# The first batch's attention written out in another order, with its loads and some copies out of PSUM moved

## The chip, the cores and the metric

The kernel runs on one core of one Trainium2 chip. The metric is device time in microseconds (us) of one execution; smaller is better. The core has five engines that run side by side, each through its own list of instructions in order: TensorE (PE, with its weight loads as PEld), VectorE (DVE), ScalarE (ACT), GpSimd (POOL) and SyncE (SP, which here only issues DMA transfers). An instruction that waits for another engine or for a transfer holds up everything behind it on its own engine.

## What is computed

Three layers in fp32, one after the other: a windowed attention, a gated feed-forward layer (FFN), and a mixture of experts. The reference, cut to what matters:

```python
# attention: q, k, v are (4 batches, 8 heads, 576, 64)
rel = pos[:, None] - pos[None, :]
scores = scale * q @ k.T ; scores = where((rel >= 0) & (rel < 64), scores, -1e9)
x = softmax(scores) @ v                      # per batch: 576 x 512
# FFN: w_in 512x1024, conv_w 3x1024, w_out 1024x512
h = maximum(x @ w_in, 0)
conv_out = sum(conv_w[k] * hp[:, k:k + S] for k in range(3))
x = (h * sigmoid(conv_out)) @ w_out
# experts: each row goes to one of 8 experts, chosen by its logits and a running gate
out[b, s] = p[e] * (maximum(x[b, s] @ w1[e], 0) @ w2[e])
```

The FFN's weights arrive as 64-bit floats; integer operations on VectorE turn them into fp32.

## The kernel before

**The stages.** For each batch b there are an attention over four pairs of heads, an FFN first layer `ffn(b)` of eight column blocks f, and output tiles `ffn_out`. The attention of batch b+1 is mixed into the FFN of batch b. The experts follow at the end. Before all that stands the attention of batch 0, which has no FFN to run beside. This document calls it the opening. The FFN of batch 0 begins with the first matmul of L470.

**The opening** is written out by hand as a string of tokens, `FIRST`, which `attention_first` reads from left to right inside a manual schedule. Each token issues its instructions on its engine, so the string sets the order on all engines at once. The digit after the letter is the pair i (0 to 3 are batch 0; 4 is the first pair of batch 1), or, for c, h and u, the chunk of the weight w_in. The second digit is the part g.

| token | work | engine |
|---|---|---|
| T, S, A, V | transposes of k (part 0), q (1) and their rests (2); scores; transposes of the softmax; products with v | PE |
| k, q, t | copies of these transposes out of PSUM | DVE (k, t) and ACT (q) |
| R | mask and row maximum of the scores, reading PSUM | DVE |
| E | exponentials | ACT |
| N, M | the softmax's division, first a third, then the rest | DVE |
| a, x | copies of A and V out of PSUM | ACT |
| l | rest of V's result after rounding, reading PSUM | DVE |
| c | three integer steps on a chunk of w_in (L597, L599, L601) | DVE |
| h, u | rounded chunk; the rest after rounding (L704) | ACT; POOL |
| v, Z | shifted copy of v; clearing of the q buffer of the next batch, after which `load_pair` issues its loads | POOL |
| D | matmuls on constants, which keep PE active | PE |
| w, W, Y | the convolution's taps | DVE, PE, DVE |

**The loads.** `load_pair(b, hp)` issues nine DMAs for a pair (k, q, their rests, v), nearly all on SP's queue; `stage_chunk(i)` loads chunk i of w_in, 512 KB, into a buffer of its own. Before the string is read, pair 0, pair 1, chunks 0 and 1 (on ACT's queue), pair 2, chunk 2, pair 3 and chunk 3 are issued. Eight transfers are outstanding at a time: a DMA on SP waits until the one that stood eight places ahead has landed.

**What the order outside the opening depends on.** The rest of the program is ordered by a scheduler, which can also put instructions of the FFN between those of the opening on an engine whose list has room.

Of the kernel before, what the change touches and what calls it, by code (L numbers as in the profile page):

```python
# [8 lines left out]
F32 = mybir.dt.float32  # L9
# [4 lines left out]
AF = mybir.ActivationFunctionType  # L14
ALU = mybir.AluOpType
# [6 lines left out]
def kernel(  # L22
# [14 lines left out]
    nc = tc.nc  # L37
# [61 lines left out]
    if True:  # L99
# [85 lines left out]
        def stage_T(b, hp, part):  # L185
            qt, kt, ta, v0, v1 = qkv[b, hp]
            qbd, kT = qbds[hp % 2], kTs[hp % 2]
            qT = hb[hp % 2][:, 1:S + 1]
            if b >= TV:

                def turn():
                    if part == 0:
                        nc.vector.transpose(kT, kt)
                    elif part == 1:
                        for h in (0, 64):
                            nc.vector.transpose(qbd[h:h + 64, :, h:h + 64], qt[h:h + 64].rearrange("p (c w) -> p c w", w=W))

                return turn
            ps = bank(b)
            if part == 2:  # L200
                nc.tensor.transpose(ps[:, 0:P], ta.rearrange("p h d -> p (h d)"), ident)

                def evict():
                    nc.vector.tensor_copy(kT[:, 512:576], ps[:, 64:128])
                    if b == 0:
                        nc.vector.tensor_copy(qT[:, 512:576], ps[:, 0:64])
                    else:
                        nc.vector.tensor_copy(qbd[0:64, 8, 0:64], ps[0:64, 0:64])
                        nc.vector.tensor_copy(qbd[64:128, 8, 64:128], ps[64:128, 0:64])

                return evict
            src = (kt, qt)[part]
            for n in range(4):
                nc.tensor.transpose(ps[:, n * P:(n + 1) * P], src[:, n].rearrange("p h d -> p (h d)"), ident)

            def evict():
                if part == 0:
                    nc.vector.tensor_copy(kT[:, 0:512], ps)
                    return
                if b == 0:  # L220
                    nc.scalar.activation(qT[:, 0:512], ps, AF.Copy)
                    return
                pv = ps.rearrange("p (c w) -> p c w", w=W)
                for h in (0, 64):
                    nc.scalar.activation(qbd[h:h + 64, 0:8, h:h + 64], pv[h:h + 64], AF.Copy)

            return evict
# [177 lines left out]
        def attention_first(ORDER, others):  # L405


            later = {}
            for t in ORDER.split():
                s_, i, g = t[0], int(t[1]) if len(t) > 1 else 0, int(t[2]) if len(t) > 2 else 0  # L410
                b, hp = divmod(i, NP)
                if s_ == "T":
                    later["kqt"[g], i] = stage_T(b, hp, g)
                elif s_ == "S":
                    later["R", i, g] = stage_S(b, hp, g)
                elif s_ == "E":
                    stage_E(b, hp, g)
                elif s_ == "N":
                    stage_N(b, hp, ((1, 3),))
                elif s_ == "M":  # L420
                    stage_N(b, hp, ((3, 9),))
                elif s_ == "A":
                    later["a", i, g] = stage_AT(b, hp, g)
                elif s_ == "V":
                    later["x", i, g], later["l", i, g] = stage_AV(b, hp, g)
                elif s_ == "v":
                    shift_v(hp)
                elif s_ in "kqt":
                    later.pop((s_, i))()
                elif s_ in "Raxl":  # L430
                    later.pop((s_, i, g))()
                else:
                    others(s_, i, g)
            assert not later
# [203 lines left out]
        def conv_out(kk):  # L638
# [18 lines left out]
            return finish  # L657

        FIRST = """
            T00 k0 T01 q0 S00 S01 R00 v0 T02 E00 R01 t0 S02 w E01 T10 R02 W T11 k1 E02 c00 T12 t1 c01 q1 v1 N0 S10 S11  # L660
            c02 M0 A00 h0 T20 a00 u0 c10 A01 c11 a01 c12 R10 h1 v2 k2 E10 R11 u1 Y D9 D6 V00 E11 V01 c20 A02 c21 T21
            x00 x01 T22 l00 S12 a02 l01 q2 t2 V02 R12 S20 x02 c22 E12 Z0 T30 l02 T31 R20 T32 S21 h2 N1 v3 E20 S22 M1
            u2 A10 k3 a10 A11 a11 t3 V10 R21 q3 V11 x10 c30 A12 x11 S30 l10 a12 l11 E21 c31 V12 c32 R22 x12 h3 l12 S31
            E22 R30 u3 S32 R31 E30 T40 N2 T41 T42 M2 A20 a20 R32 E31 V20 k4 A21 A22 t4 c40 x20 a21 l20 a22 c41 V21 E32
            V22 c42 c50 x21 N3 x22 q4 l21 l22 h4 M3 D9 D9 A30 a30 u4 c51 V30 A31 c52 x30 A32 a31 l30 a32 V31 h5 V32
            x31 u5 x32 l31 l32 Z1
        """

        with tc.manual_schedule():
# [11 lines left out]
            def stage_chunk(i, eng=nc.sync):  # L681
                c, kk = divmod(i, KD)
                early[c, kk] = load_chunk(st_p.tile([P, CC, 2], U32, name=f"raw{i}"), chunk_in(c, kk), eng)

            for i in range(2):
                stage_chunk(i, nc.scalar)
            for i in range(2, KD):
                load_pair(0, i)
                stage_chunk(i)
            part = {}  # L690

            def others(s_, i, g):

                c, kk = divmod(i, KD)
                fs = slice(c * CC, (c + 1) * CC)
                if s_ == "c":
                    if g == 0:
                        part[i] = cv.tile([P, CC], F32, name="lf")
                    bits64(early[c, kk], part[i], (g,))
                elif s_ == "h":  # L700
                    cin.pop(0)
                    nc.scalar.activation(winH[:, kk, fs], part[i], AF.Copy)
                elif s_ == "u":
                    nc.gpsimd.tensor_tensor(winL[:, kk, fs], part[i], winH[:, kk, fs].bitcast(F32), op=ALU.subtract)  # L704
                elif s_ == "w":
                    part["f"] = cv.tile([P, CC], F32, tag="lf", name="cf")[0:KC, 0:P]
                    bits64(taps, part["f"])
                elif s_ == "W":
                    part["ps"] = bank(0)
                    nc.tensor.transpose(part["ps"][:, 0:KC], part["f"], ident[0:KC, 0:KC])  # L710
                elif s_ == "Y":
                    nc.vector.tensor_copy(cw.rearrange("p k f -> p (k f)"), part["ps"][:, 0:KC])
                elif s_ == "D":
                    warm(bank(0), i)
                else:
                    nc.gpsimd.memset(qbds[i], 0.0)
                    load_pair(1, i)
                    if i == 0:
                        stage_chunk(4)
                        stage_chunk(5)  # L720

            attention_first(FIRST, others)

# [856 lines left out]
```

## Time and profile before

| | |
|---|---|
| median of 3 runs | 627.13 us (625.53 to 628.46) |
| profiled execution | 626.18 us, of which the span shows 624.5 us |
| PE busy | 593.2 us, 95% of the span |
| DVE busy | 431.0 us, 69% |
| ACT busy | 386.9 us, 62% |
| POOL busy | 221.7 us, 36% |
| first matmul of the FFN | 55.79 us after the span's start |

The span runs from the first instruction to the last in one profiled execution. PE is busy nearly throughout; the first 56 us are where it is not. The shares are averages over stages with different limits, so the opening has to be read by itself.

### The profile page before, as it was taken

Reading aid. Unit: us, or ns where it says so; the run is one execution under the profiler, and the core shown is the slowest. Engines: PE = TensorE matmul, PEld = TensorE weight load, DVE = VectorE, ACT = ScalarE, POOL = GpSimd, SP = SyncE. Lnnn points to the kernel's source line nnn. Section 1 sums busy time; section 2 is a strip of 40 time slices with the busy share of each in tenths; the row PEclk is TensorE's granted clock in tenths of the full one; section 3 lists DMA queues with packets and bytes.
Section 4 is the critical chain, followed back from the end, with each engine's and each line's share of the span. In section 5 each row is a group of like instructions: output and inputs, shape, how many; then the busy total and the mean of one; then the engine's idle time right before and its main releaser. Section 6 shows DMA issues by size and latency. Waiting matters only on the chain.

```text
span 624.5 us, 12744 instructions
## 1 busy us (share of the span) xinstructions
PE 593.2 (95%) x4503; PEld 533.9 (85%) x4503; DVE 431.0 (69%) x986; ACT 386.9 (62%) x910; POOL 221.7 (36%) x251
## 2 busy tenths in 40 slices
PE   6779999999999999999999989999999999999996
PEld 4658998899999999989987879979899799897774
DVE  4888999645786167852786977658766686576863
ACT  3567778535876357853661556566765676667863
POOL 3412000001223012342250257458567385643740
PEclk9789999799999999999999999999999999999999
DMA  8794515653245201129102289768668763524850
GB/s 188 187 233 120 165 59 114 111 130 82 53 83 100 70 35 37 35 64 273 46 2 34 93 242 358 265 223 292 218 219 307 247 222 123 179 69 144 295 174 16
DMA packets 122614, 92.17 MB, mean 148 GB/s; under 512 B 96594, under 2 KB 97170, under 8 KB 122544
## 3 DMA queue, kind: packets, MB, share of 16 engines
q1 hardware_dynamic: 116064, 79.61, 44.4%
q0 software_dynamic: 4992, 10.24, 4.9%
q10 hardware_dynamic: 1488, 1.44, 0.8%
q8 instruction: 37, 0.61, 0.4%
q14 instruction: 33, 0.27, 0.1%
HBM read 89.53 MB, written 10.71 MB: 161 GB/s over the span
## 4 chain that ended last, share of the span: by engine, by line
PE 61%; DVE 13%; ACT 9%; DMA 9%; issue 5%; SPq 2%; POOL 0%; POOLq 0%; DVEq 0%; ACTq 0%
PE psM L470 14%; PE psO L512 13%; PE psH L1327 8%; PE psO L1362 8%; PE psA L247 3%; PE psO L1341 3%; ACT x L1168 3%; DMA raw<-in_moe_w_dram 3%; PE psA L324 2%; DMA pcur<-p_dram,gidx 2%; PE psA L299 2%; DMA qk<-in_q_dram 2%; DMA raw<-in_moe_w_out_dram 1%; ACT woutH L1168 1%; PE psG L582 1%
## 5 line engine op out<-in xcount | busy, mean ns | idle before, releaser
L499 POOL TENSOR_TENSOR gL<-h,gH 128x64 fp32r<-128x64 f32 (+5 forms) x46 | 43.6, 956 | 216.0 <-ACT gH L498 209.2
L470 PE MATMUL psM<-x,winH 128*128 128x288 f32 x512 | 108.4, 303 | 0.1
L470 PEld LDWEIGHTS psM<-x,winH 128*128 128x128 f32 x512 | 82.0, 189 | 2.4 <-ACT x L334 0.4
L470 PE MATMUL psM<-x,winL 128*128 128x288 f32 x256 | 76.0, 297 | 0.0
L512 PE MATMUL psO<-woutH,gH 128*128 128x262 f32 (+2 forms) x240 | 64.4, 314 | 1.2 <-ACT gH L498 1.0
L512 PE MATMUL psO<-woutL,gH 128*128 128x262 f32 (+2 forms) x240 | 62.2, 305 | 0.0
L512 PE MATMUL psO<-woutH,gL 128*128 128x262 f32 (+2 forms) x240 | 61.2, 304 | 0.0
L1253 POOL DMA_INDIRECT out_dram<-o,sidx x24 | 31.6, 1319 | 79.6 <-ACT o L1295 41.6
L271 ACT ACTIVATE sS<-sS,mx 128x128 f32<-128x128 f32 (+1 forms) x144 | 55.1, 386 | 6.9 <-DVE mx L259 6.8
L1172 DVE TENSOR_TENSOR woutL<-raw,woutH 128x1024 fp32r<-128x1024 f32 x28 | 33.8, 1224 | 29.1 <-ACT woutH L1168 29.1
L1172 DVE TENSOR_TENSOR x<-raw,x 128x1024 fp32r<-128x1024 f32 x42 | 49.9, 1222 | 4.0 <-ACT x L1168 3.8
L1362 PE MATMUL psO<-gH,x 128*128 128x288 f32 x240 | 51.3, 296 | 0.0
L1327 PE MATMUL psH<-gH,woutH 128*128 128x288 f32 x160 | 48.3, 302 | 0.4 <-DVE gL L1330 0.4
L470 PEld LDWEIGHTS psM<-x,winL 128*128 128x128 f32 x256 | 48.4, 189 | 0.1
L1327 PE MATMUL psH<-gL,woutH 128*128 128x288 f32 x160 | 47.4, 296 | 0.0
L1327 PE MATMUL psH<-gH,woutL 128*128 128x288 f32 x160 | 47.3, 295 | 0.0
L512 PEld LDWEIGHTS psO<-woutH,gH 128*128 128x128 f32 x240 | 41.0, 190 | 4.1 <-ACT gH L498 1.6
L1168 ACT ACTIVATE x<-raw 128x1024 fp32r<-128x1024 f32 x42 | 43.0, 1056 | 0.0
L512 PEld LDWEIGHTS psO<-woutL,gH 128*128 128x128 f32 x240 | 41.4, 191 | 1.4
L512 PEld LDWEIGHTS psO<-woutH,gL 128*128 128x128 f32 x240 | 40.9, 191 | 1.2
L259 DVE CUSTOM_DVE_ANT_0 sS<-psA,mask 128x128 f32<-128x128 f32 (+1 forms) x126 | 28.8, 277 | 17.9 <-PE psA L247 15.1
L1362 PEld LDWEIGHTS psO<-gH,x 128*128 128x128 f32 x240 | 39.8, 189 | 0.0
(395 smaller groups left out, 1645.5 us busy)
## 6 DMA issues: line engine op xcount, KB each, us to landing
raw<-in_moe_w_dram SPq DMA_DIRECT2D x104, 512.0 KB
v<-in_v_dram SPq DMA_DIRECT2D x56, 128.0 KB
y_dram<-ysb SPq DMA_DIRECT2D x17, 256.0 KB
raw<-in_moe_w_out_dram SPq DMA_DIRECT2D x8, 512.0 KB
raw<-in_moe_w_dram SPq DMA_DIRECT2D x32, 128.0 KB
raw<-in_moe_w_in_dram SPq DMA_DIRECT2D x6, 512.0 KB
qk<-in_k_dram SPq DMA_DIRECT2D x32, 72.0 KB
qk<-in_q_dram SPq DMA_DIRECT2D x32, 72.0 KB
```

The source lines that it names most:

```text
L247: nc.tensor.matmul(ps[:, j * P + lo:(j + 1) * P], qbd[:, c, :], kT[:, k0:W * (c + 1)], start=True, stop=True)
L259: nc.vector.tensor_tensor_reduce(sS[:, c, lo:P], ps[:, j * P + lo:(j + 1) * P], mask[:, lo:P], -scale, -NEG, op0=ALU.add, op1=ALU.min, acc ...
L271: nc.scalar.activation(sS[:, c, lo:P], sS[:, c, lo:P], AF.Exp, scale=-1.0, bias=mx[:, c:c + 1], accum_out=sume[:, c:c + 1],)
L470: nc.tensor.matmul(ps[:, 0:HS], wt[:, kk, f * P:(f + 1) * P], xt[:, c0:c0 + HS], start=n == 0, stop=n == 3 * KD - 1,)
L499: e1.tensor_tensor(gL[:, f, r:r + m], t[:, done:done + m], gH[:, f, r:r + m].bitcast(F32), op=ALU.subtract)
L512: nc.tensor.matmul(p_[:, 0:cs.stop - cs.start], gt[:, kk, r:r + P], wt[:, kk, cs], start=n == 0, stop=n == 3 * KF - 1,)
L1168: nc.scalar.activation(dst[kk][0], raws[kk], AF.Copy)
L1172: nc.vector.tensor_tensor(L_, raws[kk], H_.bitcast(F32), op=ALU.subtract)
L1253: nc.gpsimd.indirect_dma_start(out=out[:, :], out_offset=bass.IndirectOffsetOnAxis(ap=sidx[0:n, c:c + 1].bitcast(U32), axis=0), in_=o[0:n] ...
L1327: nc.tensor.matmul(ps, a, w, start=n == 0, stop=n == 3 * KD - 1)
L1341: nc.tensor.matmul(ps, a[:, f], w, start=n == 0, stop=n == 3 * KF - 1)
L1362: nc.tensor.matmul(ps, a, w[:, f], start=n == 0, stop=n == 3 * KF - 1)
```

## The change

It replaces the string `FIRST` by another order of nearly the same tokens. Of the matmuls on constants (D) 3 remain of 33. Copies of k out of PSUM go to ACT for every pair but the first, in batch 1 also inside the FFN's stage, where the small copies of part 2 go to ACT as well; the copy of q for pair 1 goes to DVE (token Q1). Chunk 1 is loaded on SP behind pair 1, and chunks 4 and 5 directly behind chunk 3 instead of behind the first loads of batch 1.

```diff
                 def evict():
-                    nc.vector.tensor_copy(kT[:, 512:576], ps[:, 64:128])
                     if b == 0:
+                        nc.vector.tensor_copy(kT[:, 512:576], ps[:, 64:128])
                         nc.vector.tensor_copy(qT[:, 512:576], ps[:, 0:64])
                     else:
-                        nc.vector.tensor_copy(qbd[0:64, 8, 0:64], ps[0:64, 0:64])
-                        nc.vector.tensor_copy(qbd[64:128, 8, 64:128], ps[64:128, 0:64])
+                        nc.scalar.activation(kT[:, 512:576], ps[:, 64:128], AF.Copy)
+                        nc.scalar.activation(qbd[0:64, 8, 0:64], ps[0:64, 0:64], AF.Copy)
+                        nc.scalar.activation(qbd[64:128, 8, 64:128], ps[64:128, 0:64], AF.Copy)
...
-            def evict():
+            def evict(dve=b + hp + part == 0):
+                if dve and (part == 0 or b == 0):
+                    nc.vector.tensor_copy((kT, qT)[part][:, 0:512], ps)
+                    return
                 if part == 0:
-                    nc.vector.tensor_copy(kT[:, 0:512], ps)
+                    nc.scalar.activation(kT[:, 0:512], ps, AF.Copy)
                     return
...
-            T00 k0 T01 q0 S00 S01 R00 v0 T02 E00 R01 t0 S02 w E01 T10 R02 W T11 k1 E02 c00 T12 t1 c01 q1 v1 N0 S10 S11
+            T00 k0 T01 q0 S00 c00 S01 T02 R00 T10 T11 c01 R01 t0 c02 S02 w D3 Q1 E00 W T12 E01 k1 R02 h0 t1 S10 S12
...
-            for i in range(2):
-                stage_chunk(i, nc.scalar)
+            stage_chunk(0, nc.scalar)
+            stage_chunk(1)
             for i in range(2, KD):
                 load_pair(0, i)
                 stage_chunk(i)
+            for i in range(KD, KD + 2):
+                stage_chunk(i)
...
-                    if i == 0:
-                        stage_chunk(4)
-                        stage_chunk(5)
```

**SP, behind the loads of pair 1's q.** The names are those of the tiles: `qk_164` holds k and q of pair 1, `v0_165` and `v1_166` its v, `qk2_180` k and q of pair 2, `raw1_178` chunk 1. Before:

```order
L151 DMA qk_164<-in_q_dram 128x4x64 x2
L152 DMA qk_164<-in_q_dram 64x2x64
L153 DMA qk_164<-in_k_dram 64x2x64
L168 DMA v0_165<-in_v_dram 128x4x64 x2
L165 DMA v1_166<-in_v_dram 64x2x64
L151 DMA qk2_180<-in_k_dram 128x4x64 x2
```

And now:

```order
L168 DMA v0_165<-in_v_dram 128x4x64 x2
L165 DMA v1_166<-in_v_dram 64x2x64
L616 DMA raw1_178<-in_moe_w_in_dram 128x1024
L151 DMA qk2_180<-in_k_dram 128x4x64 x2
L151 DMA qk2_180<-in_q_dram 128x4x64 x2
```

Chunk 1 has moved from ACT's queue, where it was issued beside pair 0, to a place behind all of pair 1.

**PE, where pair 1 begins.** `qk_147` is pair 0, `qk_164` pair 1; matmuls that read `kT0` are scores of pair 0. Before:

```order
L250 MATMUL psM_230<-kT0_128,h_125 64x128 x6
L201 MATMUL psA_242<-ident_62,qk_147 128x128
L250 MATMUL psO_252<-kT0_128,h_125 64x128 x6
L214 MATMUL psA_266<-ident_62,qk_164 128x128 x4
L710 MATMUL psM_274<-ident_62,cf_259 128x24
L214 MATMUL psA_276<-ident_62,qk_164 128x128 x4
```

And now:

```order
L254 MATMUL psM_236<-kT0_128,h_125 64x128 x6
L201 MATMUL psA_243<-ident_62,qk_147 128x128
L215 MATMUL psO_248<-ident_62,qk_164 128x128 x4
L215 MATMUL psA_253<-ident_62,qk_164 128x128 x4
L254 MATMUL psM_265<-kT0_128,h_125 64x128 x6
```

Both transposes of pair 1 have moved ahead of the last scores of pair 0, which now wait behind them on PE.

**DVE, around the first chunk.** `lf` is a chunk on its way from 64 bits to fp32, `cf` the taps, `sS,mx` what R writes. Before, the chunk's first two steps stood behind R of pair 0:

```order
L218 COPY kT1_129<-psA_266 128x512
L597 TENSOR_SCALAR lf_285<-raw0_176 128x512
L204 COPY kT1_129<-psO_287 128x64
L206 COPY h_125<-psO_287 128x64
L599 SCALAR_TENSOR_TENSOR lf_285<-raw0_176,lf_285 128x512
L280 TENSOR_SCALAR sume_222<-sume_222 128x9
```

And now the chunk's last step stands ahead of pair 0's last R (which reads `psM_265`):

```order
L206 COPY h_125<-psA_243 128x64
L607 SCALAR_TENSOR_TENSOR lf_234<-raw0_176,lf_234 128x512
L603 TENSOR_SCALAR cf_272<-cr_160 24x128
L605 SCALAR_TENSOR_TENSOR cf_272<-cr_160,cf_272 24x128
L607 SCALAR_TENSOR_TENSOR cf_272<-cr_160,cf_272 24x128
L219 COPY h_125<-psA_253 128x512
L263 ISA sS_224,mx_225<-psM_265,mask_67 128x128
```

All of chunk 0 has moved ahead, the copy of k for pair 1 is gone from DVE, and the copy of its q (L219 into `h_125`) has come.

## Rows read from the trace of the kernel before

**Rows 1.** By stage: busy PE, PEld, DVE, ACT, POOL; PEclk, DMA share, GB/s.

```profile
13.40:55.79 42.39, 33.29 (x366) 26.32 (x367) 37.06 (x127) 26.80 (x99) 13.22 (x14) 0.84 0.78 192
55.79:117.80 62.01, 58.51 (x498) 54.64 (x494) 60.03 (x156) 48.26 (x135) 1.02 (x2) 1.00 0.45 114
117.80:124.60 6.80, 6.80 (x33) 6.73 (x33) 2.07 (x14) 3.20 (x16) 0.00 (x0) 0.50 0.58 88
```

**Rows 2.** PE in order of time, end of the opening: start, us, what.

```profile
53.76 1.61 PE L247 MATMUL psA<-kT,qbd 128*128 128x64 f32 x12
...
55.79 0.40 PE L470 MATMUL psM<-x,winH 128*128 128x288 f32 x1
```

**Rows 3.** PE, where pair 1 begins; idle time ahead in brackets.

```profile
12.73 0.63 PE L214 MATMUL psA<-ident,qk 128*128 128x128 f32 x4 [0.63 <-DMA qk<-in_k_dram]
...
13.73 0.30 PE L214 MATMUL psA<-ident,qk 128*128 128x128 f32 x1 [0.20 <-DMA qk<-in_q_dram]
```

**Rows 4.** SP's issues of q, pairs 1 and 2; the stage 5:10.

```profile
8.09 2.70 SPq L151 DMA_DIRECT2D qk<-in_q_dram  x2
...
15.17 1.05 SPq L151 DMA_DIRECT2D qk<-in_q_dram  x2
...
5.00:10.00 5.00, 4.31 (x32) 3.59 (x31) 1.35 (x7) 1.35 (x6) 0.72 (x3) 1.00 1.08 261
```

**Rows 5.** DVE and POOL in order of time, opening.

```profile
14.78 0.68 DVE L599 SCALAR_TENSOR_TENSOR lf<-raw,lf 128x512 uint32<-128x512 uint32 x1
16.18 0.41 DVE L284 TENSOR_TENSOR sS<-sS,sume 128x256 f32<-128x256 f32 x1
18.29 0.41 DVE L597 TENSOR_SCALAR lf<-raw 128x512 uint32<-128x512 uint32 x1
18.74 1.64 DVE L599 SCALAR_TENSOR_TENSOR lf<-raw,lf 128x512 uint32<-128x512 uint32 x1
24.87 1.45 DVE L597 TENSOR_SCALAR lf<-raw 128x512 uint32<-128x512 uint32 x1 [1.88 <-DMA raw<-in_moe_w_in_dram]
31.48 1.50 DVE L284 TENSOR_TENSOR sS<-sS,sume 128x256 f32<-128x256 f32 x1
38.77 0.29 DVE L259 CUSTOM_DVE_ANT_0 sS<-psM,mask 128x128 f32<-128x128 f32 x1
50.25 1.76 DVE L599 SCALAR_TENSOR_TENSOR lf<-raw,lf 128x512 uint32<-128x512 uint32 x1
...
38.75 1.28 POOL L704 TENSOR_TENSOR winL<-lf,winH 128x512 fp32r<-128x512 f32 x1 [6.05 <-ACT winH L702]
50.11 1.36 POOL L704 TENSOR_TENSOR winL<-lf,winH 128x512 fp32r<-128x512 f32 x1 [10.08 <-ACT winH L702]
```

**Rows 6.** Copies out of PSUM: groups (count, busy, mean ns), 55.79:117.8; one of ACT.

```profile
L218 DVE COPY kT<-psA 128x512 f32<-128x512 f32 x3 | 2.0, 681 | 0.0
L209 DVE COPY qbd<-psA 64x64 f32<-64x64 f32 x3 | 0.7, 227 | 0.1
L305 ACT ACTIVATE aT<-psA 64x128 f32<-64x128 f32 x2 | 0.5, 264 | 0.6 <-PE psA L299 0.6
...
14.39 0.60 ACT L221 ACTIVATE h<-psA 128x512 f32<-128x512 f32 x1 [0.57 <-PE psA L214]
```

**Rows 7.** Stretches of the opening at half clock; PE's waits ahead of two.

```profile
15.50:18.80 3.30, 3.30 (x26) 2.97 (x23) 3.20 (x8) 1.17 (x3) 1.79 (x3) 0.50 0.74 166
22.30:25.60 3.30, 2.65 (x13) 1.90 (x14) 1.42 (x8) 1.72 (x10) 2.93 (x4) 0.50 0.84 209
42.80:49.50 6.70, 6.28 (x54) 4.70 (x53) 4.66 (x16) 5.63 (x22) 0.00 (x0) 0.50 0.71 171
...
22.95 2.10 PE L181 MATMUL psM<-ident 128*128 128x256 bf16 x9 [3.65 <-DVE mx L259]
42.57 0.27 PE L297 MATMUL psA<-ident,sS 128*64 128x128 f32 x1 [2.57 <-DVE mx L259]
```

**Rows 8.** PE's waits, 55.79:117.8: us in total, times, longest.

```profile
PE psW L652 <- ACT wt L649: 1.9, 4, 0.6
```

More of the change, by code (lines that the diff above doesn't have):

```diff
@@ L429, in attention_first @@
                     later.pop((s_, i))()
+                elif s_ in "KQ":
+                    later.pop((s_.lower(), i))(True)
                 elif s_ in "Raxl":
@@ L659 @@
         FIRST = """
-            T00 k0 T01 q0 S00 S01 R00 v0 T02 E00 R01 t0 S02 w E01 T10 R02 W T11 k1 E02 c00 T12 t1 c01 q1 v1 N0 S10 S11
[L661 to L666, printed above, removed]
+            T00 k0 T01 q0 S00 c00 S01 T02 R00 T10 T11 c01 R01 t0 c02 S02 w D3 Q1 E00 W T12 E01 k1 R02 h0 t1 S10 S12
+            S11 Y T20 T22 T21 E02 R10 R12 N0 M0 A00 A02 A01 u0 t2 E10 k2 q2 c10 R11 S20 c11 E12 a00 R20 E11 v0 S21 a01
+            V00 S22 E20 R21 N1 V01 a02 R22 A10 E21 V02 c12 T30 M1 c20 T31 x02 A11 x00 v2 l00 x01 T32 k3 v1 l01 c21 a10
+            q3 t3 A12 S30 l02 E22 Z0 S32 S31 h1 a11 c22 R30 N2 R31 E30 u1 M2 c30 h2 V10 a12 x10 A21 R32 V11 c31 l10 v3
+            E31 E32 V12 c32 Z1 A20 A22 u2 c40 a20 h3 V20 N3 c41 A30 M3 x11 a22 x12 a21 x20 V22 a30 x22 u3 A32 l11 l12
+            V21 l20 c50 A31 V30 c42 a32 V32 x21 c51 a31 l21 l22 V31 x30 T40 c52 h4 x32 T41 x31 T42 k4 h5 l32 q4 l31
+            l30 u4 t4 u5
         """
@@ L702, in others @@
                     nc.scalar.activation(winH[:, kk, fs], part[i], AF.Copy)
-                elif s_ == "u":
-                    nc.gpsimd.tensor_tensor(winL[:, kk, fs], part[i], winH[:, kk, fs].bitcast(F32), op=ALU.subtract)
+                elif s_ in "uU":
+                    e = nc.vector if s_ == "U" else nc.gpsimd
+                    e.tensor_tensor(winL[:, kk, fs], part[i], winH[:, kk, fs].bitcast(F32), op=ALU.subtract)
                 elif s_ == "w":
```

## The prediction

> **What bounds the kernel now.** I read the busy times by stage first, then each engine's list in order of time with its waits, then the lines by group. Behind 124.6 us PE has hardly a gap, and the instruction lists of before and of the changed kernel are the same there from early in the second FFN on; what the change can give is the time at which PE gets to that work. The opening is where PE is not the bound. From 13.4 us, when the loads of pair 1 have come, to the FFN's first matmul at 55.79 us [rows 2] VectorE is busy 37.06 of 42.39 us, PE 33.29 (12.23 of it at half clock) and ScalarE 26.80 [rows 1, 7]. So VectorE's list sets the opening, and PE waits for it, 3.65 and 2.57 us at a time [rows 7]. In the FFN's stage, 55.79 to 117.8, VectorE (60.03 of 62.01 us) and PE (58.51) are both nearly full [rows 1].
>
> Part of VectorE's busy time is no work. The second integer step on a chunk takes 0.68 us, but 1.64 and 1.76 us where a subtraction of GpSimd had begun just before; the first step takes 0.41 and once 1.45, the division's first third 0.41 and once 1.50 [rows 5]. These four cost 0.96 + 1.08 + 1.04 + 1.09 = 4.2 us. Beside the subtraction at 38.75 the row maximum, which reads PSUM, took its usual 0.29 us [rows 5]. The change tries to put the subtractions there.
>
> **Loads.** SP's two issues of pair 1's q took 2.70 us, those of pair 2 1.05 [rows 4]: they wait for earlier transfers to land, two chunks of 512 KB among them. PE's transposes of pair 1 waited for data until 12.73 and 13.73 us [rows 3]. With chunk 1 behind pair 1, 512 KB less lie ahead, at 261 GB/s [rows 4] 2.0 us. So pair 1's q should be there at about 11.7 us. The last scores of pair 0 now wait for that on PE; before, they could begin as soon as pair 0 was complete. They end at about 12.7, and the last row maximum of pair 0 on VectorE at 13.4 instead of 12.9. That costs half a microsecond, while chunk 0's three steps, done from about 8 us in time that VectorE had free, take 2.1 us out of the later list. If chunk 0 lands late, it holds up the first row maximum by up to about 1 us; nothing in the rows shows its landing, and I put it at zero.
>
> **VectorE's list from 13.4 us.** From 37.06 us go: four copies of k, 4 x 0.68 = 2.7 [rows 6]; the small copies of batch 1's first pair, 3 x 0.22 = 0.7 [rows 6]; chunk 0, 2.1; and FFN work that stood in the opening and now stands behind it (chunk 6 with its subtraction and the first row maxima of batch 1, 0.41 + 3 x 0.68 + 3 x 0.29 = 3.3, the steps from [rows 5], the subtraction taken as one of them). That leaves 28.3 us, of which 4.2 are the stretched instructions. 24.1 us is the list if all subtractions find a read of PSUM, 28.3 if they collide as now; q of pair 1 on VectorE comes before 13.4.
>
> A rule of the Trainium skill (SBUF — State Buffer, section Who interferes with whom) says that a VectorE instruction with at most one SBUF input, outside the two-port modes, does not contend with GpSimd, and that otherwise the one that starts first keeps the port until its end. By it every subtraction beside a row maximum would be free, and the list 24.1 us; that the new order meets these moments rests on it starting each subtraction when planned, which no row shows.
>
> **ScalarE's list** gets the copies of k at 0.60 each and three small ones at 0.26 [rows 6]. Of 26.80 us, q of pair 1 (0.60) goes, and chunk 6 and exponentials that now come later (about 1.1); k of pairs 2, 3 and 4 (1.8), the small copies (0.8) and most of pair 0's last exponentials (0.9, which now start later) come. That is 28.6 us, and 25 up to the last copy of x that the FFN needs, since its last entries (k, q and the small ones of pair 4, a chunk) are not needed for it.
>
> **PE's list** at full clock is 33.29 - 12.23 / 2 = 27.2 us [rows 1, 7]. The 33 matmuls on constants go; nine took 2.10 us at half clock [rows 7], so 33 are 3.9 at full clock. Batch 1's first scores (1.61 us with what runs beside them [rows 2]) go behind the FFN's first matmuls. That leaves 21.7 us.
>
> **The opening's new end.** The three lists end at the earliest at 13.4 + 24.1 = 37.5 (VectorE), 38.4 (ScalarE) and 35.1 (PE). VectorE lost 5.3 us to waits before; with these and every collision it ends at 47.0, with neither at 37.5. Three lists of nearly equal length that hand work to each other in turn lose more to waits than one long one with two short ones, and PE may be at half clock for a part, so I stay at the upper end: the FFN begins at **47.0 us**, 8.8 us earlier. Bounds: 42 and 52.
>
> **What of it reaches the end.** PE has to make up batch 1's first scores, 1.6 us. VectorE has 3.3 us more to do in the FFN's stage, and 3 x (0.68 + 3 x 0.22) = 4.0 less for the k copies of the next three pairs [rows 6], so it is as full as before and does not hold the stage back. PE's gaps there, 3.5 us of which 1.9 are waits for ScalarE's copy `wt` [rows 1, 8], may shrink or grow with ScalarE's 48.26 us + 4.2 (the same three pairs, 3 x 1.4) + 1.1. I count half of the 1.6 us as lost: 8.8 - 0.8 = **8.0 us**. The profiled execution goes from 626.18 to 618.2; the median of the runs shown is 0.95 higher, so 627.13 goes to **619.1 us**. The later loads (chunks 4 and 5, batch 1's first pairs) are issued earlier with their buffers, and I count nothing for them.
>
> **Rivals.**
>
> *The clock stays at half (slower).* Each of the three half-clock stretches of the opening comes with waits of PE, two of them with those of 3.65 and 2.57 us, and the matmuls on constants stand just there [rows 7]; now 30 of them are gone, the 18 ahead of the FFN among them. If PE ran at half clock throughout, its 21.7 us would be 43.4 and the FFN begin at 56.8, 1.0 us later than now; with 1.6 us of scores to make up and a stretch such as that of 117.8 to 124.6, 6.8 us at half clock [rows 1], in the FFN's first matmuls, 3.4 us more: 627.1 + 6.0 = 633. Without gain it ends where the FFN begins at 50.8, 5.0 us before now: PE's list would take 37.4 us, with about three quarters of its work at half clock. Against it: at half clock PE is busier, and in each stretch of the opening it came back to full clock. The Trainium skill (TensorE: Matmul & The Clock Gate, Part 1) says that half rate is the default and activity releases it; the rows agree as far as that each stretch began after PE stood idle. Chance 0.07.
>
> *ScalarE swallows it.* In the FFN's stage ScalarE goes from 48.3 to 53.6 of 62 us, and what PE waits for longest there comes from it [rows 8]. If its idle time of 13.8 us stays as it is, since it waits for others in turn, the stage takes 67.4 us instead of 62.0 and 5.4 of the 8.8 us are gone: 627.1 - 8.8 + 5.4 = 623.7, with the late scores 625. For it: ScalarE's work stands between matmuls everywhere. Against: VectorE and PE were the full ones. Chance 0.20.
>
> *The collisions end and the waits too.* The FFN begins at 42: 627.1 - 13.8 + 1.6 = 615, and 611.5 if the half-clock stretch at 117.8 also goes (3.4 us). Chance 0.17.
>
> *The new order does nothing for the opening*: VectorE's list without the moved work is what it was, and collisions and waits grow by what the copies saved. The FFN begins at 52 and with the late scores 625 is left. Chance 0.06.
>
> **The numbers.** My forecast, the FFN at 45 to 50 us and most of it kept, holds 616 to 622.5: chance 0.50. The range must reach to the ScalarE rival above and most of the tight case below: 612 to 625.5. About 0.5% (3.1 us) is what a measurement can tell from no change. Faster than 624.0: 0.50 + 0.17 + about half of the ScalarE rival and a little of the last, 0.79. Slower than 630.3: most of the clock rival, 0.05. Same: 0.16.
>
> **What would show it.** In the profile after: the FFN's first matmul at 45 to 50 us; pair 1's transposes of q near 11.7; no integer step or division of more than 1 us beside a subtraction, or at most two; PE's half-clock stretches in the opening no longer than 13 us in all; in the FFN's stage VectorE still over 90% busy and PE's waits for ScalarE below 5 us. I am wrong if the FFN begins after 52, if its stage has grown by more than 3 us, or if most of the opening shows half clock.

## The result, and the profile after

The changed kernel takes **618.79 us** (median of 4 runs, 618.61 to 619.55), the kernel before 627.47 in the same comparison (625.53 to 628.46). The comparison puts the ratio of the times at 0.9886, with a 95% interval of 0.9862 to 0.991; the two medians alone would give 0.986. A second comparison, with more runs of each, gave 0.9907 (0.9883 to 0.993). Predicted were 619.1 us, within 612.0 to 625.5. The profiled execution is the slowest of the first four: 619.55 us, with a span of 617.8.

The first group below answers [rows 1]: the changed kernel by stage. The last two stretches cut the time behind the FFN's first matmul at one mark, the end of ScalarE's last relu (L483, L477 before) of batch 1's FFN. From there on these two kernels need the same, 437.0 and 437.3 us, so that between them everything is decided ahead of the mark. The other kernels of this study need 436 to 440 us there in their single profiles, so a stretch up to the mark tells their end to a few us only. Columns as in [rows 1].

```profile
13.40:46.79 33.39, 26.71 (x321) 21.41 (x318) 28.40 (x114) 24.58 (x97) 13.41 (x15) 0.80 0.85 214
46.79:108.80 62.01, 55.55 (x462) 53.62 (x461) 57.79 (x149) 51.76 (x148) 1.57 (x2) 0.96 0.47 119
46.79:180.82 134.03, 127.48 (x1123) 122.23 (x1122) 102.63 (x286) 97.57 (x303) 11.10 (x14) 0.97 0.47 105
180.82:617.80 436.98, 423.50 (x2977) 379.55 (x2975) 287.01 (x546) 264.10 (x514) 195.19 (x204) 1.00 0.49 157
```

The same cut in the kernel before:

```profile
55.79:187.24 131.45, 127.95 (x1111) 121.51 (x1108) 102.83 (x289) 91.13 (x282) 10.54 (x14) 0.97 0.44 100
187.24:624.50 437.26, 423.33 (x2977) 379.68 (x2975) 286.90 (x546) 263.76 (x515) 192.08 (x204) 1.00 0.49 156
```

The FFN begins 9.0 us earlier, at 46.79 instead of 55.79. From there to the mark it takes 134.03 instead of 131.45 us, so 2.6 us are given back, and 6.4 reach the mark. What is given back is idle time of PE: 134.03 - 127.48 = 6.5 us against 131.45 - 127.95 = 3.5, at the same mean clock of 0.97. PE's busy time did not grow, though 12 matmuls more stand in this stretch, the first scores of batch 1.

PE in order of time, the rows that answer [rows 2] and [rows 3], idle time ahead in brackets:

```profile
10.83 1.05 PE L215 MATMUL psO<-ident,qk 128*128 128x128 f32 x4
11.78 0.63 PE L215 MATMUL psA<-ident,qk 128*128 128x128 f32 x4
...
17.43 0.63 PE L215 MATMUL psA<-ident,qk 128*128 128x128 f32 x4 [1.35 <-DMA qk<-in_k_dram]
...
19.21 1.06 PE L215 MATMUL psA<-ident,qk 128*128 128x128 f32 x4
...
34.51 0.52 PE L303 MATMUL psA<-ident,sS 128*128 128x128 f32 x3 [2.96 <-DVE sS L288]
...
46.79 0.51 PE L476 MATMUL psM<-x,winH 128*128 128x288 f32 x2
...
69.73 0.59 PE L518 MATMUL psO<-woutH,gH 128*128 128x262 f32 x1 [3.02 <-ACT gH L504]
```

SP's issues of q for pairs 1 and 2, which answer [rows 4]:

```profile
7.33 1.25 SPq L151 DMA_DIRECT2D qk<-in_q_dram  x2
...
13.42 1.06 SPq L151 DMA_DIRECT2D qk<-in_q_dram  x2
```

Pair 1's issue takes 1.25 us instead of 2.70, and the pair is there in time; it is pair 2 that PE now waits for. The wait at 69.73 is new. The copies that went to ScalarE (groups of 13.4 to 108.8: count, busy, mean ns) take there what [rows 6] gave for them:

```profile
L222 ACT ACTIVATE kT<-psA 128x512 f32<-128x512 f32 x5 | 3.0, 593 | 2.4 <-PE psA L215 2.4
L208 ACT ACTIVATE kT<-psA 128x64 f32<-128x64 f32 x3 | 0.7, 227 | 0.0
```

VectorE and GpSimd where they meet, which answers [rows 5]:

```profile
24.18 0.55 DVE L284 TENSOR_SCALAR sume<-sume 128x9 f32<-128x9 f32 x1
30.78 1.05 DVE L284 TENSOR_SCALAR sume<-sume 128x9 f32<-128x9 f32 x1
34.62 0.28 DVE L263 CUSTOM_DVE_ANT_0 sS<-psO,mask 128x128 f32<-128x128 f32 x1
35.25 1.13 DVE L605 SCALAR_TENSOR_TENSOR lf<-raw,lf 128x512 uint32<-128x512 uint32 x1
38.12 1.50 DVE L288 TENSOR_TENSOR sS<-sS,sume 128x256 f32<-128x256 f32 x1
45.77 0.36 DVE L341 TENSOR_TENSOR x<-psA,x 128x192 fp32r<-128x192 f32 x1 [1.19 <-ACT x L338]
48.10 1.66 DVE L607 SCALAR_TENSOR_TENSOR lf<-raw,lf 128x512 uint32<-128x512 uint32 x1
...
23.64 1.06 POOL L725 MEMSET qbd<- 128x1152 f32 x1
30.54 1.27 POOL L713 TENSOR_TENSOR winL<-lf,winH 128x512 fp32r<-128x512 f32 x1 [5.83 <-ACT winH L710]
34.30 1.54 POOL L713 TENSOR_TENSOR winL<-lf,winH 128x512 fp32r<-128x512 f32 x1
38.01 1.32 POOL L713 TENSOR_TENSOR winL<-lf,winH 128x512 fp32r<-128x512 f32 x1 [2.18 <-ACT winH L710]
45.59 1.28 POOL L713 TENSOR_TENSOR winL<-lf,winH 128x512 fp32r<-128x512 f32 x1 [6.26 <-ACT winH L710]
```

A subtraction stands where the plan wanted it, beside a read of PSUM, at 45.59 us (L341, 0.36 us as always). Three others, at 30.54, 34.30 and 38.01, still met VectorE on SBUF, and at 24.18 VectorE met the clearing of a buffer (the memset at 23.64). With undisturbed durations of 0.17, 0.17, 0.68 and 0.41 us, the four instructions at 24.18, 30.78, 35.25 and 38.12 lost 0.38 + 0.88 + 0.45 + 1.09 = 2.8 us; the one at 48.10 comes behind the FFN's begin. The row maximum at 34.62 kept its 0.28 us beside a subtraction.

Stretches at half clock, which answer [rows 7]:

```profile
18.50:21.90 3.40, 2.93 (x14) 2.81 (x14) 1.92 (x10) 1.72 (x7) 1.01 (x2) 0.51 0.80 194
35.60:45.80 10.20, 9.14 (x97) 6.89 (x93) 8.94 (x20) 6.32 (x21) 1.76 (x3) 0.50 0.87 205
69.70:73.10 3.40, 3.37 (x15) 3.34 (x16) 3.40 (x6) 2.12 (x5) 0.00 (x0) 0.51 0.34 135
107.30:110.70 3.40, 3.40 (x41) 2.93 (x41) 3.40 (x7) 2.31 (x6) 0.00 (x0) 0.50 0.74 120
```

The opening has 13.6 us of it, as much as before; the long one begins a microsecond after PE's wait of 2.96 us.

PE's waits from the FFN's begin to the mark (in total, times, longest), which answer [rows 8]:

```profile
PE psO L518 <- ACT gH L504: 3.7, 2, 3.0
PE psW L658 <- ACT wt L655: 2.8, 2, 1.6
```

### The profile page after: what moved, and what is told of

The parts are those of the page before. It is cut to its first block, busy times and chain, and to the rows that moved or that the text cites. A ratio compares the mean times of both kernels' runs of the same rounds, so it can differ in the third digit from the quotient of the medians.

```text
span 617.8 us, 12686 instructions
## 1 busy us (share of the span) xinstructions
PE 586.7 (95%) x4473; PEld 529.9 (86%) x4473; DVE 423.4 (69%) x968; ACT 391.7 (63%) x928; POOL 224.7 (36%) x251
## 4 chain that ended last, share of the span: by engine, by line
PE 66%; DVE 11%; ACT 8%; DMA 7%; issue 5%; SPq 2%; POOL 0%; POOLq 0%; ACTq 0%; DVEq 0%
PE psM L476 14%; PE psO L518 13%; PE psH L1333 10%; PE psO L1368 9%; PE psO L1347 4%; PE psA L328 3%; PE psA L251 3%; ACT x L1174 3%; PE psA L303 2%; DMA pcur<-p_dram,gidx 2%; DMA raw<-in_moe_w_dram 1%; PE psG L588 1%; DMA h<-y_dram,gidx 1%; PE psX L1289 1%; ACT woutH L1174 1%
## 5 line engine op out<-in xcount | busy, mean ns | idle before, releaser
L518 PE MATMUL psO<-woutL,gH 128*128 128x262 f32 (+2 forms) x240 | 63.8, 305 | 0.0
L518 PE MATMUL psO<-woutH,gL 128*128 128x262 f32 (+2 forms) x240 | 62.5, 302 | 0.0
```

Source lines behind the costliest of these rows:

```text
L518: nc.tensor.matmul(p_[:, 0:cs.stop - cs.start], gt[:, kk, r:r + P], wt[:, kk, cs], start=n == 0, stop=n == 3 * KF - 1,)
```

## The experiments

Each is a kernel timed against the kernel before on one chip. The median of the kernel before was 625.5 to 626.0 us there, so ratios are compared, not times. "FFN" is the start of its first matmul in the one profiled execution, which can lie several us from the median of its own kernel (that of `old_loads` took 619.86 us, the median is 623.55); ratios decide, profiles show where.

### The three parts, singly and in pairs

The change falls into the string (order), the loads and the engines of the copies. `order_only`, `loads_only` and `copies_only` put one of them into the kernel before; `old_loads` and `old_copies` take one out of the changed kernel; `after_again` is the changed kernel itself. The edits are the diff's own parts: for the loads

```diff
-            for i in range(2):
-                stage_chunk(i, nc.scalar)
+            stage_chunk(0, nc.scalar)
+            stage_chunk(1)
...
+            for i in range(KD, KD + 2):
+                stage_chunk(i)
...
-                    if i == 0:
-                        stage_chunk(4)
-                        stage_chunk(5)
```

and for the copies back on VectorE in `old_copies` (the small ones likewise)

```diff
-            def evict(dve=b + hp + part == 0):
+            def evict(dve=part == 0):
...
-            ... S02 w D3 Q1 E00 W ...
+            ... S02 w D3 q1 E00 W ...
```

Expected of `after_again`:

> The changed kernel once more, as a yardstick beside the others of this call. Its first runs gave 0.9886 of the time before, with an interval of 0.9862 to 0.991. If a trace can be taken at its word, the FFN begins at 46.8 us again. If the place of the half-clock stretches differs from one execution to the next, it begins anywhere from 44.5 to 48.5, as it did in kernels whose opening is the same, and single profiles tell nothing below 2 us.

Of `order_only`:

> The new string alone, with every load issued and every copy made where it was. By the prediction's sum of VectorE's list, the copies are worth 2.7 us of the opening and the loads 2: the FFN begins at 51 to 52 us, and the time is about 0.996 of the time before. If the order alone carries the gain of the opening, as the run with the old copies suggests (the FFN at 46.6 us there): FFN at 47 to 49 us and 0.994 to 0.997, the rest lost to VectorE's copies in the FFN's stage. If the three parts only work together: FFN at 54 or later, no gain.

Of `loads_only`:

> The kernel before with only the loads issued in the new order. The old string still puts pair 1's transposes behind pair 0's scores. If the arrival of pair 1's q holds back the opening by itself, the FFN begins 1.5 to 2 us earlier, at about 54 us: 0.997. If the loads are worth something only beside the new string: 0.999 to 1.001, FFN at 55.3 to 56.3. If chunk 1, which the old string wants at 18 us, now comes late: FFN at 56.5 to 58 and 1.002.

Of `copies_only`:

> The kernel before with only the copies of k (all but pair 0's) and batch 1's small ones moved to ScalarE. If VectorE's list sets the opening, 3.4 us less of it bring the FFN to 52.4 us, and 4.0 us less in the FFN's stage help besides: 0.990 to 0.995. If the order sets the opening, the FFN stays at 55 to 56 us; what is then gained is the FFN's stage alone, which the pair of runs with and without these copies puts at about 3 us: 0.995. If ScalarE swallows it: 0.999 to 1.003.

Of `old_loads`:

> The changed kernel with the loads issued where they were: chunk 1 on ScalarE's queue ahead of pair 1, chunks 4 and 5 behind batch 1's first loads. If pair 1's q sets the begin of the list, its transposes come at 13.7 us instead of 11.8, pair 0's last row maximum 1.5 to 2 us later, and the FFN at 48.5: 620.5 us. If the loads are hidden behind other work: FFN within 0.5 us of 46.8, 618.5 to 619.2 us. If chunk 1 behind pair 1 does harm, since it delays pair 2, for which PE waits 2.3 us between 16 and 19 us in the changed kernel: those waits go and the time is 617.

Of `old_copies`:

> The changed kernel with every copy out of PSUM on the engine where it was: k and batch 1's small ones on VectorE, q on ScalarE. If VectorE's list sets the opening, four copies of k at 0.68 us and three small ones at 0.22 come back and one copy of q at 0.68 goes, 2.7 us: the FFN begins at about 49.5 us. In the FFN's stage VectorE gets 4.0 us more at 93% busy. Together 621.5 to 625.5 us. If the order alone gives the gain: FFN within 1 us of 46.8 and at most 620 us. If ScalarE holds the FFN's stage back: PE's waits for its copies there (7.7 us in the changed kernel) fall by half or more, and what the opening loses is given back, 617 to 620 us.

Measured (the clock is the mean granted clock over all executions of that kernel):

| kernel | order | loads | copies | ratio to before (95% interval) | FFN, us | clock |
|---|---|---|---|---|---|---|
| before | old | old | old | 1 | 55.79 | 0.988 |
| `loads_only` | old | new | old | 0.9961 (0.9941 to 0.9981) | 54.98 | 0.987 |
| `copies_only` | old | old | new | 1.0013 (0.9992 to 1.0035) | 59.90 | 0.983 |
| `order_only` | new | old | old | 1.0043 (1.002 to 1.0067) | 49.66 | 0.979 |
| `old_copies` | new | new | old | 0.9942 (0.9921 to 0.9963) | 46.61 | 0.985 |
| `old_loads` | new | old | new | 0.9966 (0.9947 to 0.9985) | 48.42 | 0.988 |
| `after_again` | new | new | new | 0.9907 (0.9883 to 0.993) | 47.25 | 0.986 |

The three parts alone add up to 0.0043 - 0.0039 + 0.0013 = 0.2% slower; together they are 0.9 to 1.1% faster. The order alone brings the FFN 6.1 us forward and still ends later. Its stretch from the FFN's begin to the mark shows where that goes:

```profile
49.66:188.46 138.80, 131.65 (x1123) 125.32 (x1122) 106.17 (x304) 93.28 (x287) 11.45 (x14) 0.95 0.43 98
```

and in PE's order of time its longest wait there:

```profile
71.95 0.58 PE L517 MATMUL psO<-woutH,gH 128*128 128x262 f32 x1 [3.59 <-ACT gH L503]
```

138.80 us against 131.45 before: PE idles 7.15 us instead of 3.50, and is busy for 131.65 instead of 127.95, at a clock of 0.95 instead of 0.97 and with 12 matmuls more, the first scores of batch 1. PE came to the FFN earlier than what the FFN needs next, and waited. Here that was work of VectorE and hardly a load: from the FFN's begin to 72 us VectorE is busy 21.23 of 22.34 us, with the old copies among its work, and the only load that it waits for is this one:

```profile
DVE lf L602 <- DMA raw<-in_moe_w_out_dram: 1.0, 1, 1.0
```

The mean clock of its executions, 0.979, is the lowest of all. A slower kernel was in none of the three cases expected of `order_only`.

The loads are worth 0.4% alone, with the FFN only 0.8 us earlier, 1.0% beside the new order (1.0043 to 0.9942) and 0.6 to 0.8% beside order and copies. (`old_loads` begins the FFN at 48.42 us, as expected, but loses more in the end than the 1.7 us put for it.) The copies are worth 0.8% beside the new order (1.0043 to 0.9966), 0.35 to 0.56% when the loads are new too, and nothing alone. Of this the opening shows nothing: with every copy back on VectorE the FFN begins at 46.61 us. The expectation that VectorE's list would then be 2.7 us longer and the FFN at 49.5 is wrong: up to the FFN's begin VectorE is busy 28.73 us instead of 28.40. Only nine of the twelve rests of V's result (token l) stand ahead of that begin now, so the FFN's first matmul does not mark the end of VectorE's list. In the old order the copies on ScalarE even delay the FFN, to 59.90, though from there to the mark it takes 125.28 us instead of 131.45 (in one of its fastest executions, 624.52 us). The time came out as the third case put it, ScalarE swallowing the gain, but not by a full list of ScalarE. PE waits in the opening for a copy of A, and ScalarE issues that copy late because a chunk of the FFN, which the scheduler has put ahead of it, waits for VectorE:

```profile
55.34 0.63 ACT L633 ACTIVATE winH<-lf 128x512 fp32r<-128x512 f32 x1 [2.30 <-DVE lf L605]
...
56.62 0.57 PE L328 MATMUL psA<-aT,v 128*64 128x64 f32 x12 [2.27 <-ACT aT L312]
```

### Copies in the FFN's stage back on VectorE

```diff
-            def evict(dve=b + hp + part == 0):
+            def evict(dve=b + hp + part == 0 or b * hp > 0 and part == 0):
```

and the small copies of the same three pairs. Expected:

> The changed kernel with the copies of k and the small copies of batch 1's last three pairs, which all stand in the FFN's stage, back on VectorE; the opening stays. If VectorE holds the FFN's stage, where it is 93% busy, 4.0 us of work more lengthen it by 2 to 4 us: 621 to 623 us. If ScalarE swallows part of the gain there, PE's waits for it (4.4 us for the copy of the transposed weights and 3.7 for the rounded h) shrink to about 3 and the time falls by 1 to 3 us: 616 to 618. If neither engine is the bound there: 618.8 within 0.7.

Measured: 0.9942 (0.9915 to 0.9969), the same as with all copies on VectorE. So 0.35 to 0.56% (2.2 to 3.5 us) is what the copies give, and as far as the intervals tell it comes from the 4.0 us of copies in the FFN's stage alone; those of the opening are worth nothing that can be measured. The intervals of this run and the changed kernel's overlap a little; two runs agree on it. ScalarE does not swallow the gain: relieved of this work, the kernel gets slower, not faster. (The expectations put PE's waits for ScalarE in the changed kernel at 7.7 and 8.1 us; the rows above have 6.5.)

The opening of this kernel has the string, the loads and the copies of the changed kernel, yet the FFN begins at 44.86 us instead of 46.79 and 47.25. One profile's begin of the FFN is uncertain by about 2 us.

### Matmuls on constants put back

Three places where PE stands idle get 36 matmuls:

```diff
-            S11 Y T20 T22 ...  x10 A21 R32 ...  c41 A30 M3 ...
+            S11 Y D9 T20 T22 ...  x10 D9 D9 A21 R32 ...  c41 D9 A30 M3 ...
```

> The changed kernel with matmuls on constants where PE stands idle: nine ahead of pair 2's first transposes, eighteen in the wait of 2.96 us ahead of the transposes at 34.5 us, nine in the wait of 0.93 us at 39.7. If the clock theory holds for this part, the half-clock stretch from 35.6 to 45.8 us goes or shrinks; PE is busy there without a gap from 39.7 us on, 7.1 us at half clock, so that the FFN begins up to 3 us earlier: 615.5 to 617 us. If VectorE's list sets the opening, PE only waits longer for the copies of x: FFN within 1 us of 46.8, 618 to 619.5 us. If the matmuls on constants have to wait for their banks: later than 47.5 and 620.

Measured: 0.9909 (0.9884 to 0.9934). The opening, and the rest to the mark:

```profile
13.40:44.45 31.05, 25.85 (x356) 20.71 (x354) 28.10 (x113) 24.18 (x97) 12.60 (x15) 1.00 0.87 220
44.45:177.72 133.27, 127.47 (x1123) 122.16 (x1122) 102.85 (x288) 97.51 (x303) 11.75 (x14) 0.97 0.48 109
```

The clock part is confirmed: full clock from 13.4 us to the FFN, which begins at 44.45. The time put with it, 615.5 to 617 us, did not come: in the time this kernel can't be told from the changed one. Behind the FFN's begin 133.27 us follow, and waits for the rounded h of 3.5 us in all, against 3.7. So PE's speed in the opening was not what limited the whole.

### The late chunk

In the changed kernel VectorE waits for chunk 7 at 55 us. VectorE in order of time in `after_again`, with the wait and the FFN's own h (L497) queued behind it:

```profile
56.03 0.43 DVE L603 TENSOR_SCALAR lf<-raw 128x512 uint32<-128x512 uint32 x1 [1.20 <-DMA raw<-in_moe_w_in_dram]
56.38 0.81 DVE L497 SCALAR_TENSOR_TENSOR h<-h,cw 128x576 f32<-128x576 f32 x1
```

SP issued that chunk late, behind loads of batch 1's pairs:

```profile
51.71 0.53 SPq L616 DMA_DIRECT2D raw<-in_moe_w_in_dram  x1
```

The queue is not all of it. The chunks behind chunk 5 share two buffers with those of w_out. In the changed kernel's profile VectorE's last step on chunk 6, the stretched one at 48.10, ends at 49.76, and only then is a buffer free for chunk 7, which SP issues at 51.53. So the loads ahead of it cost 1.8 us at most. Nor is the wait new: VectorE waits for this chunk in the kernel before too, where PE waits 0.8 us at most for the rounded h.

```profile
DVE lf L597 <- DMA raw<-in_moe_w_in_dram: 1.0, 1, 1.0
```

`early_67` loads chunks 6 and 7 into the buffers of chunks 0 and 1, and so takes them out of the queue's late part and out of the two shared buffers:

```diff
-                early[c, kk] = load_chunk(st_p.tile([P, CC, 2], U32, name=f"raw{i}"), ...
+                early[c, kk] = load_chunk(st_p.tile([P, CC, 2], U32, name=f"raw{i % 6}"), ...
...
                     load_pair(1, i)
+                    if i == 0:
+                        stage_chunk(6)
+                        stage_chunk(7)
```

> The changed kernel with chunks 6 and 7 of w_in loaded into the buffers of chunks 0 and 1 as soon as these are free, issued behind the loads of batch 1's first pair instead of later ones; the scheduler orders the FFN's stage anew around them. In the changed kernel's traces VectorE waits 1.2 to 2.1 us for chunk 7 at 55 us with the first block's h queued behind it, and PE then waits 2 to 3 us for the rounded h at 60 to 70 us, with a half-clock stretch of 3.4 us behind it. If this late transfer is what takes back gain in the FFN's stage, VectorE's wait goes, PE's idle time there falls from 4.8 to 6.5 us to 3 to 4, and the ratio to the time before goes from 0.9886 and 0.9907 to 0.983 to 0.987. If the FFN's stage is bound by VectorE's amount of work, as the run with the copies on VectorE suggests (4.0 us of work, 3 us of time): 0.987 to 0.991, with PE's waits only moved. If the earlier 1 MB delays pair 5's loads: 0.991 to 0.995 and PE waits for qk at 50 to 56 us.

`early_67_warm` has the 36 matmuls besides:

> The run with chunks 6 and 7 loaded early, and the 36 matmuls on constants besides, which kept the whole opening at full clock and brought the FFN's begin from 46.8 to 44.5 us without a measurable gain in the end. If the late chunk is what held the FFN's stage, the 2.3 us now reach the end as well: 0.979 to 0.985. If the amount of VectorE's work holds it, no better than the run without the matmuls, within 0.002.

Measured: 0.9847 (0.9815 to 0.9879) and 0.9813 (0.9781 to 0.9845), both as the late chunk's theory says. In `early_67` SP issues both chunks at 40.27 us:

```profile
40.27 1.85 SPq L616 DMA_DIRECT2D raw<-in_moe_w_in_dram  x2
```

The stretch to the mark is 129.11 us, with PE idle for 4.11 and the full clock throughout:

```profile
46.39:175.50 129.11, 125.00 (x1123) 119.41 (x1122) 101.99 (x286) 97.54 (x303) 10.92 (x14) 1.00 0.48 107
```

and of PE's waits that for the rounded h has shrunk to 0.5 us:

```profile
PE psW L658 <- ACT wt L655: 2.7, 5, 0.8
PE psA L301 <- DVE sS L286: 0.6, 1, 0.6
PE psO L518 <- ACT gH L504: 0.5, 1, 0.5
```

PE idles 2.4 us less than in the changed kernel and is busy 2.5 us less, at the full clock. The edit moves more than chunk 7: with the shared buffers free, the second chunk of w_out, which the changed kernel issues at 53.24 us, goes out here beside the first:

```profile
36.77 1.07 SPq L616 DMA_DIRECT2D raw<-in_moe_w_out_dram  x2
```

The scheduler, which knows of the earlier loads, also ordered the FFN's stage anew. How much of the gain is the landing of chunk 7, of the chunk of w_out, or that order was not separated. The amount of VectorE's work was not the only limit there: it is the same (101.99 us busy against 102.63 in the changed kernel), and the time fell.

The 36 matmuls gave nothing measurable by themselves. On top of the early chunks the ratio falls by another 0.0034. The intervals of the two ratios overlap, but both kernels ran beside each other on one chip, and there all six executions with the matmuls (612.63 to 615.77 us) are faster than all five without (616.00 to 617.56), by 2 us in the median. So once the chunks are early, the matmuls are worth something. Where, one profile of each does not show: the FFN begins at 46.39 and 46.20 us, the mark follows 129.11 and 129.09 us later, and the 2.0 us by which the two differ come behind it.

`early_67_warm13` has 13 instead of 6 matmuls on constants at the very start:

```diff
-            warm(bank(0), 6)
+            warm(bank(0), 13)
```

> The run with chunks 6 and 7 early and the 36 matmuls on constants, with 13 instead of 6 matmuls on constants at the very start, in the 2.0 us in which PE waits for the first k. In the profile without them, four transposes at 5 us took 1.09 us and still did so at 12.0, and 0.60 only from 19.7 on; in other kernels that change came between 11 and 17 us. If the time without work before 5.0 us is what sets the late rise to full clock, it now comes by 8 to 12 us, the first scores end up to 3 us earlier and the FFN begins at 43.5 to 45: 0.976 to 0.981. If it is the first scores and waits behind them, the rise stays at 11 to 20 us and the ratio at 0.979 to 0.984. If they delay pair 0's transposes, the opening begins later and 0.982 to 0.985.

Measured: **0.9809** (0.9784 to 0.9833), 612.85 to 614.69 us in six runs. Its interval lies below both of the changed kernel's: this version beats both kernels. Against 0.9813 without the seven matmuls the difference is not measurable. Its first matmuls and pair 1's transposes:

```profile
1.54 2.96 PE L181 MATMUL psM<-ident 128*128 128x256 bf16 x13 [1.54 <-POOL ident masks.py:199]
4.91 1.09 PE L215 MATMUL psA<-ident,qk 128*128 128x128 f32 x4 [0.41 <-DMA qk<-in_k_dram]
...
11.76 0.63 PE L215 MATMUL psA<-ident,qk 128*128 128x128 f32 x4 [0.28 <-DMA qk<-in_q_dram]
```

The transposes are at 0.63 us by 11.76 and no longer at 1.09 as at 4.91, but so they were in the changed kernel's own profile (11.78); in `early_67_warm` they took 1.09 still at 11.99. One profile each does not show that the seven matmuls made the difference.

### Subtractions in halves

```diff
-                    e.tensor_tensor(winL[:, kk, fs], part[i], winH[:, kk, fs].bitcast(F32), op=ALU.subtract)
+                    for a in (0, 256):
+                        hs = slice(c * CC + a, c * CC + a + 256)
+                        e.tensor_tensor(winL[:, kk, hs], part[i][:, a:a + 256], winH[:, kk, hs].bitcast(F32), op=ALU.subtract)
```

> The changed kernel with each of the opening's six subtractions on GpSimd as two instructions of 256 columns. If a VectorE instruction that meets one waits until the one in progress ends, each meeting costs up to about 0.65 us instead of up to 1.1; the five meetings in the changed kernel's trace (0.4 to 1.0 us, 3.5 in all) shrink to about half, VectorE's list is 1.5 us shorter and the FFN begins 0.5 to 1.5 us earlier, 0.987 to 0.989. If VectorE gets no turn between the halves, or meets both: no change, 0.989 to 0.992.

Measured: 0.9906 (0.9876 to 0.9937), no change. Instead of four instructions stretched by 0.3 us or more ahead of the FFN there are seven, three of them these (the one at 24.37 beside the memset of a buffer):

```profile
24.37 0.85 DVE L286 TENSOR_SCALAR sS<-sS,sume 128x64 f32<-128x64 f32 x1
30.69 0.64 DVE L286 TENSOR_SCALAR sS<-sS,sume 128x64 f32<-128x64 f32 x1
38.04 0.81 DVE L286 TENSOR_SCALAR sS<-sS,sume 128x64 f32<-128x64 f32 x1
```

This shape takes 0.25 us undisturbed. Each meeting costs less (at most 0.6 instead of 1.1), but there are more of them, 3.6 us in all against 2.8. Smaller pieces do not help; whether no meeting at all would, was not tried.

## Why the prediction was right, and where it was not

**The opening's end: right (47.0 predicted, 46.79 and 47.25 measured), its make-up only in part.** The lists came out near the forecast: VectorE 28.40 us where 28.3 with every collision was put (that the two agree to 0.1 us is partly luck: 2.8 us are collisions, not 4.2, and 25.6 the rest, not 24.1), ScalarE 24.58 where 25 was put up to the last copy of x, PE 26.71, of which 12.07 lie in the half-clock stretches, so 20.7 at full clock where 21.7 was put. But the copies, 3.4 us of the sum, do not set the begin: with them back it is 46.61. So the step "VectorE's list sets the opening" does not hold in the way it was used, with each us of the list a us of the opening. What sets the begin is the order (6.1 us alone) and, beside it, the loads (49.66 to 46.61 with the old copies, 48.42 to about 47 with the new; single profiles, good to 2 us).

**Collisions: not ended.** I named as the sign of the plan's success at most two stretched instructions of over a microsecond. There are three ahead of the FFN and one behind. The list's upper end was the right one to take, though not all of it was made of collisions.

**Loads: timing right, worth mis-sized.** Pair 1's q came at 11.78 us (11.7 predicted), and chunk 0 held nothing up. The loads' part as a whole is worth 0.6 to 1.0% beside the new order, 3.7 to 6.3 us, of which the opening shows 1 to 3; the sum had 2 us for chunk 1 and "I count nothing" for chunks 4 and 5 and the later loads. How the worth divides between these was not separated, but a part behind the opening, put at nothing, is there. Beside the old copies it shows as a higher clock: 135.33 us from the FFN's begin to the mark instead of 138.80, at a clock of 0.99 instead of 0.95, with PE idle as long as before (7.04 us, 7.15 with the old loads). Beside the new copies the profiles do not show it (133.29 us with the old loads, 134.03 and 132.38 with the new), and that of `old_loads` shows its fastest execution.

**What reaches the end: the loss was undersized.** I took 0.8 us of 8.8 as lost. In the profiled pair 2.6 of 9.0 are lost, not to batch 1's late scores but to PE's waits, most of them for the first blocks' rounded h. That h stands on VectorE's list behind chunks of the weights, which VectorE is busy with, or waits for, when PE comes early; loading the chunks earlier takes most of the waits for h away. With the opening 0.2 better and this 1.8 worse than put, the profiled pair differs by 6.6 us (626.18 and 619.55) instead of 8.0; the medians differ by 8.7, and the two ratios stand for 5.8 and 7.2 us. The forecast lies among them; that it came within 0.4 us of the first median is luck, since the profiled pair, from whose parts it was added up, moved by 6.6 us and not by 8.0.

**VectorE in the FFN's stage: right.** 57.79 of 62.01 us, 93%, and the 4.0 us of copies taken from it are worth 2.2 to 3.5 us. So it does hold the stage back in part, which the sum did not say. PE's waits for ScalarE there came out at 6.5 us, not below 5; the stage did not grow by more than 3.

**Rivals.** *The clock*: the opening's half-clock time is 13.6 us, just over the 13 named as its bound and no more than before, and putting 36 matmuls back removes it without a measurable gain. So it was no threat here, since what follows was not ready; with chunks 6 and 7 early, the same matmuls are worth about 2 us, in a way that the profiles do not show. *ScalarE swallows it*: ruled out for the changed kernel by the run that relieves ScalarE and gets slower. *Collisions and waits end*: neither did, and ending the clock's part alone gained nothing. *The order does nothing for the opening*: it does most of it, but alone it makes the kernel slower, which was among none of the rivals.

## What to carry to other kernels

When a bound stage is shortened, look for what the next stage needs first and when that is ready: an order that brings PE to a stage 6 us early is worth nothing if the engine that prepares its inputs is not ahead by as much, because its list is full or because a load waits for its buffer and its turn in the queue. The waits can cost clock besides: behind the wait of 3.02 us, PE's clock is at half for 3.4 us. Test the parts of a change singly and in pairs; here the sum of the single effects has the wrong sign. An engine's list that comes out at the measured length proves the sum, not that each entry of it was on the path.

## What the runs showed of the hardware that was not expected

**The first microseconds.** Ahead of the first change that the profile records, its clock row says 1.00, yet four transposes at 5 us take 1.09 us in the profiles shown, as they do at half clock (1.06 at 19.21 us in the changed kernel), and 0.60 to 0.63 later. The durations change to the short ones between 11 and 20 us, in executions of nearly the same opening at different times. Where they change late, the first scores run at the long durations, and the clock row overstates that part of the opening.

**Small instructions are stretched too.** A VectorE operation on 9 columns took 1.05 us instead of 0.17 where a subtraction of GpSimd had begun 0.24 us before; it ended with the subtraction, within 0.02 us. Row maxima and L341, which read PSUM, kept their time beside one (0.28 us at 34.62, 0.36 at 45.77). The Trainium skill (SBUF — State Buffer, section Who interferes with whom) frees VectorE instructions with one SBUF input only outside the two-port modes, into which it says this kind of operation can go; the trace agrees with that, though it does not show the mode.
